# Three kinds of reordering in the opening of a fused attention and mixture-of-experts kernel: more weight slices converted early, one batch's loads issued later, and eight matmuls of block means moved

## The chip, the cores and the metric

The kernel runs on one core of one Trainium2 chip. The metric is the device time of the whole program in microseconds (us). Shorter is better.

A core has these engines, each with its own instruction queue, worked off in the order in which the program wrote it: PE (TensorE, matmuls; its weight loads are shown apart as PEld), DVE (VectorE), ACT (ScalarE), POOL (GpSimd) and SP (SyncE, which here only issues DMA transfers).

## The reference

Three stages follow each other. The sizes: 2 batches, 8 heads, 768 positions, head width 64, so 1536 tokens of width 512.

```python
def _attn_ref(q, k, v):
    block, window = (32, 16)
    k_sum = k.reshape(B, H, nb, block, D).max(axis=3)
    v_sum = v.reshape(B, H, nb, block, D).mean(axis=3)
    ...
    scores_all = np.concatenate([scores_l_m, scores_s], axis=-1)
    a = np.exp(scores_all)
    a = a / (np.sum(a, axis=-1, keepdims=True) + 1e-09)
    v_all = np.concatenate([v, v_sum], axis=2)
    return np.matmul(a, v_all).astype(np.float32)

def _moe_ref(x, w_in, w_out):
    h = x @ w_in
    relu6 = np.clip(h + 3.0, 0.0, 6.0)
    g = h * relu6 / 6.0
    return (g @ w_out).astype(np.float32)

def _moe2_ref(x, w_gate, w1, w2):
    logits = x @ w_gate
    ...
    for e in range(E):
        mask = assigned == e
        h = np.maximum(x[mask] @ w1[e], 0.0)
        out[mask] = h @ w2[e]
```

`w_in` is 512 x 2048. Each of the 8 experts takes 192 tokens, those of the highest logits first. Each query sees the keys nearer than 16 positions and, for each block of 32 keys, the block's maximum as a key and the block's mean as a value. `w_in`, `w_out` and `w_gate` arrive as 64-bit floats and are turned into 32-bit ones on the chip.

## The kernel before

**Tiles and units.** The tokens are 12 tiles of 128 (six to a batch). Three tiles make a unit, so there are four units. Unit `u` of the first dense stage (`gemm1(u)`) is 16 slices of `w_in`, and each slice is 12 matmuls of 128x384 on PE (lines 621 to 623), an ACT instruction (line 624) and a DVE instruction (the gate, line 637). The results of two neighbouring slices use two PSUM banks in turn, so slice `f + 2` can begin only when the gate of slice `f` is done. Attention runs one unit ahead: while `gemm1(u)` runs, the attention of unit `u + 1` is threaded between its slices. Attention of unit 0 has nothing to hide behind; it is written out by hand in `prologue()`.

**Attention of one tile** is two halves of four heads. For each half: `front` (8 score matmuls, line 383, then four DVE instructions, line 391, that add the mask and take the minimum), `soften` (exponentials on ACT, line 402; sums and reciprocals on DVE, lines 404 and 405; a POOL multiplication, line 406), `turn` (four transposes, line 414, and an ACT copy) and `values` (8 matmuls, line 429, from the V window `VW`). `window(n)` makes the key window of tile `n` with two DVE copies (line 368). `q_prep` transposes a tile of q (line 353) through PSUM bank 7 or 4; `values` of the even or odd tiles use the same banks. The block means of the first batch are 8 matmuls with a constant matrix (`vsum_mul`, line 199), after which `vsum_place` copies the result into both `VW` buffers (DVE, line 203, then ACT, line 204). No `values` product can run before that.

**The slices of `w_in`.** A slice is loaded as 512 KB (`w_in_load`, line 247) into one of four raw buffers. `w_conv` makes 32-bit floats of it with three DVE instructions (`f32_ops`, run at line 272); when the third is done, the load of the slice four later is queued. `w_split` cuts the result into a high part (ACT, line 289) and a low part (POOL, line 290), two slices after the conversion in the program's order (`CLAG`). `AHEAD` slices are converted while the prologue runs, the rest during unit 0.

**What sets the order.** `drive` interleaves several generators. Each has a total and a start and an end on a common scale; after each step the generator that is least far along goes next, and the numbers that the steps yield are how far each one went. They set only the order of the program text. Here `S0` and 1.0 are the start and the end of the conversions on the scale of the prologue. SP's queue is in the same order: a load that must wait for its buffer holds every load behind it.

**The second batch.** Its k and v come through the same buffers as the first batch's q and v (`load_rows("kraw", k, 1, j)`, 4 x 256 KB in pieces of 256 bytes, line 169, and `vsum_load(1, g)`, 2 x 768 KB, line 173). They are needed at the start of unit 1.

Of the kernel before, what the change touches and what calls it, by code (L numbers as in the profile page):

```python
# [16 lines left out]
HP = H // 2  # L17
# [9 lines left out]
UT = 3  # L27
# [16 lines left out]
SEEK, COUNT = 4600, 1900  # L44
ROUTE = 100000
CLAG = 2
AHEAD = 4
EARLY = 13
LEFT = 4
VLAG = 0  # L50
VN = 3
ATTS = [31212, 20565, 23910, 18810]
END = [0.92, 0.92, 0.92]
S0 = 0.27
S1 = 0.7
LX = 4
TAIL = [0, 1], [2]
# [31 lines left out]
def build(ctx, tc, q, k, v, w_in, w_out, w_gate, w1, w2, out):  # L89
# [30 lines left out]
    def bank(i):  # L120
        return psum.tile([128, 512], FT, name=f"bank{i}")
# [35 lines left out]
    q0 = early.take([H, UT, D])  # L157
# [6 lines left out]
    def load_rows(kind, src, b, i):  # L164
        if src is k:
            x = k1[i % 4]
        else:
            x = att.tile([128, H, D], FT, name="raw", bufs=3)
        SP.dma_start(x, src[b, :, i * 128:(i + 1) * 128, :].rearrange("h s d -> s h d"))
        raw[kind, b, i] = x  # L170

    def load_first(x, src, b, hs, rs, r):
        SP.dma_start(x[:, hs, rs], src[b, hs].rearrange("h (p r) d -> p h r d", r=r)[:x.shape[0], :, rs])

    def load_v(n):

        b, i = divmod(n, 6)
        for g in range(2):
            lo = i * 128 + g * QG - W
            a, z = max(lo, 0), min(lo + WIN, S)  # L180
            SP.dma_start(VW[n % 2][a - lo:z - lo, g], v[b, :, a:z, :].rearrange("h s d -> s h d"))
# [6 lines left out]
    def vsum(b):  # L188
        m = KR // 2
        while m:  # L190
            POOL.tensor_tensor(vs[:, :, :m], vs[:, :, :m], vs[:, :, m:2 * m], op=OP.add)
            m //= 2
# [13 lines left out]
    for g in range(2):  # L206
        hs = slice(HP * g, HP * g + HP)
        for rs in RH:
            load_first(k0, k, 0, hs, rs, KR)
        load_first(q0, q, 0, hs, slice(0, UT), UT)  # L210

    for x in VW:
        POOL.memset(x, 0.0)
# [88 lines left out]
    def kprep_first(g):  # L302
        hps = slice(2 * g, 2 * g + 2)
        for i, rs in enumerate(RH):
            for hp in range(2 * g, 2 * g + 2):
                p = bank((2, 3, 5, 6)[2 * i + hp % 2])
                for j in range(4):
                    for z in range(2):
                        PE.matmul(p[64 * z:64 * z + 64, j * KP:(j + 1) * KP], k0[:, 2 * hp + z, 4 * i + j], ident[:KP, :KP],  # L309
                                  start=True, stop=True, skip_group_check=True)  # L310
                ACT.activation(kT[:, hp, rs], p[:, :4 * KP].rearrange("p (r s) -> p r s", r=4), AF.Copy)
                DVE.tensor_reduce((ks if i else kmax)[:, hp], p[:, :4 * KP].rearrange("p (r n s) -> p n r s", r=4, s=4),
                                  axis=AX.XY, op=OP.max)
                yield 450
        DVE.tensor_tensor(ks[:, hps], ks[:, hps], kmax[:, hps], op=OP.max)

    def qprep_first(g):
        for hp in range(2 * g, 2 * g + 2):
            p = bank(7 if hp % 2 else 4)
            for i in range(UT):  # L320
                for z in range(2):
                    PE.matmul(p[64 * z:64 * z + 64, i * 128:(i + 1) * 128], q0[:, 2 * hp + z, i], ident,
                              start=True, stop=True, skip_group_check=True)
            ACT.activation(qT0[:, hp].rearrange("p (s r) -> p r s", r=UT), p[:, :U].rearrange("p (r s) -> p r s", r=UT), AF.Copy)
        if g:
            for n in range(UT):
                fr[n] = qT0[:, :, n * 128:(n + 1) * 128]
# [82 lines left out]
    def turn(n, h):  # L410
        A = Abuf[(2 * n + h) % (LAG + 1)]
        p = bank(2)
        for c in range(4):
            PE.transpose(p[:KEYS, c * 128:(c + 1) * 128], A[:, c], ident)  # L414
        at = att.tile([128, 4, 128], FT, name="at", bufs=3)
        ACT.activation(at[:KEYS], p[:KEYS].rearrange("p (c s) -> p c s", c=4), AF.Copy)  # L416
        ats[n, h] = at
# [35 lines left out]
    def halves():  # L453
        for n in range(UT, NT):
            b, i = divmod(n, 6)
            if b and i == 0:
                vsum(b)
                yield from kprep(b)
                q_prep(n)
                window(n)  # L460
                yield 2400
            for h in range(2):
                t = pend.pop(0) if len(pend) >= LAG else None
                if t:
                    turn(*t)
                    turned.append(t)
                    yield 660
                after = h == 1 and i < 5
                first = (n, h) == (UT, 1)
                if not first:  # L470
                    front(n, h, after)
                    yield 1250 + 450 * after
                pend.append((n, h))
                while turned:
                    if turned[0] == (6 * b, 0):
                        vsum_mul(0, True)
                        vsum_place()
                    values(*turned.pop(0))
                    yield 1000
                emit_x()  # L480
                if first:
                    yield 1
                    front(n, h, after)
                    yield 1250 + 450 * after
                yield from soften()
                emit_x()
                if (n, h) == (UT, 0):
                    for g in range(2):
                        vsum_load(1, g)
                    for j in range(4):  # L490
                        load_rows("kraw", k, 1, j)
            if i == 5:
                while pend or turned:
                    if turned:
                        yield 700
                        values(*turned.pop(0))
                        yield 1000
                        emit_x()
                    if pend:
                        yield 800  # L500
                        t = pend.pop(0)
                        turn(*t)
                        turned.append(t)
                        yield 660

    turned = []
    attention = halves()

    def attend_unit(u):
# [264 lines left out]
    def prologue():  # L774
        soft = []

        def half(n, h, after=False):
            front(n, h, after)
            soft.append(soften())
            next(soft[-1])  # L780
            pend.append((n, h))

        def rest():
            for _ in soft.pop(0):
                pass

        def turned_one():
            t = pend.pop(0)
            turn(*t)
            turned.append(t)  # L790

        for c in kprep_first(0):
            yield c
        qprep_first(0)
        window(0, slice(0, 2))
        yield 600
        for c in kprep_first(1):
            yield c
        half(0, 0)
        yield 1250  # L800
        qprep_first(1)
        window(0, slice(2, 4))
        yield 600
        half(0, 1, True)
        rest()
        yield 1250
        def block_means(i):
            for j in range(i, i + 2):
                vsum_mul(j, j == KR - 1)

        def both(t):
            values(*t)
            emit_x()

        half(1, 0)
        rest()
        yield 1250
        block_means(0)
        yield 1700
        turned_one()  # L820
        yield 660
        block_means(2)
        yield 1700
        half(1, 1, True)
        rest()
        yield 1700
        turned_one()
        yield 660
        block_means(4)
        yield 1700  # L830
        half(2, 0)
        rest()
        yield 1250
        block_means(6)
        vsum_place()
        yield 1700
        turned_one()
        yield 660
        for i in range(2):
            both(turned.pop(0))  # L840
            yield 1000
        half(2, 1, True)
        rest()
        yield 1700
        turned_one()
        yield 660
        both(turned.pop(0))
        yield 1000
        rest()
        yield from attend_unit(0)  # L850

    w_in_load(0)
    for g in range(2):
        vsum_load(0, g)
    w_in_load(1)
    load_v(0)
    load_v(1)
    for j in range(2, NW):
        w_in_load(j)
    for n in range(2):  # L860
        load_rows("qraw", q, 0, UT + n)

    def splits():
        for s in range(NF + CLAG):
# [7 lines left out]
    splitting, second = splits(), gemm2()  # L872
    drive([[prologue(), ATTS[0], 0, 1], [part(splitting, 4 * AHEAD), 4 * AHEAD, S0, 1.0]], soon)
    tlast = late = None
    for u in range(NU):
        st = []
        if u + 1 < NU:
            st = [[attend_unit(u + 1), ATTS[u + 1], -0.02, END[u]]]
            if u == 0:
                st.append([splitting, 4 * (NF - AHEAD) + CLAG, 0.0, S1])  # L880
        else:
# [422 lines left out]
```

## Time and profile before

| | |
|---|---|
| median of 3 runs | 585.88 us (585.55 to 587.0) |
| the profiled execution: its own time | 584.98 us |
| its span in the trace, first to last instruction | 583.0 us |
| busy share of the span: PE, DVE, ACT, POOL | 94%, 61%, 50%, 28% |
| mean granted clock of TensorE | 0.981 of full speed |

The profiled execution's own time is 0.9 us under the median, and 2.0 us of it lie around the span. The prologue is the first 50.0 us of the span; the 16 slices of unit 0 follow.

### The profile page before, as it was taken

How to read it: one execution, taken by the hardware profiler on the slowest of the kernel's cores; microseconds unless marked ns; L12 is line 12 of the kernel's file. 1: busy time of each engine (PE TensorE's matmuls, PEld its weight loads, DVE VectorE, ACT ScalarE, POOL GpSimd, SP SyncE). 2: the span in 40 equal slices, each digit the busy share in tenths (PEclk: the TensorE clock that was granted, in tenths of full speed). 3: DMA queues.
4: the chain of work that ended last, by engine and by line, in shares of the span. 5: the costliest groups of instructions: out<-in, count | busy, mean ns of one | idle time of the engine just before them, and what ended most of it. 6: DMA issues, size and time to landing. Idle time of an engine off the chain costs nothing.

```text
span 583.0 us, 10815 instructions
## 1 busy us (share of the span) xinstructions
PE 548.8 (94%) x3867; PEld 458.5 (79%) x3867; DVE 356.2 (61%) x1022; ACT 291.7 (50%) x698; POOL 163.9 (28%) x197
## 2 busy tenths in 40 slices
PE   6768789989999999999999999999999999999993
PEld 6447678879889989986677777778789888988882
DVE  6577795644543288750045655553588888888880
ACT  4556464456544445561132232234576777677750
POOL 1124348111111032582244444456001100111011
PEclk9789899999999999999999999999999999999998
DMA  9978962302110145430042000004589888998811
GB/s 235 231 193 171 276 177 48 77 20 47 28 36 19 47 141 176 140 105 2 1 126 91 1 1 1 1 18 183 155 262 289 251 242 249 288 254 233 255 47 33
DMA packets 98270, 75.05 MB, mean 129 GB/s; under 512 B 38112, under 2 KB 84704, under 8 KB 98208
## 3 DMA queue, kind: packets, MB, share of 16 engines
q1 hardware_dynamic: 96224, 67.96, 43.2%
q0 software_dynamic: 1984, 6.32, 3.0%
q8 instruction: 33, 0.54, 0.4%
q14 instruction: 29, 0.24, 0.1%
HBM read 67.55 MB, written 6.71 MB: 127 GB/s over the span
## 4 chain that ended last, share of the span: by engine, by line
PE 53%; issue 27%; DVE 8%; DMA 5%; POOL 3%; ACT 2%; SPq 0%; POOLq 0%; DVEq 0%; ACTq 0%
PE bank L738 8%; PE bank L739 7%; PE bank L740 7%; PE bank L621 6%; PE bank L622 5%; PE bank L623 5%; POOL out_dram L1107 3%; DVE bank L272 2%; PE bank L649 2%; PE bank L383 2%; PE bank L199 2%; PE bank L429 2%; PE bank L414 1%; DMA big<-in_moe_w_out_dram 1%; PE bank L309 1%
## 5 line engine op out<-in xcount | busy, mean ns | idle before, releaser
L621 PE MATMUL bank<-x,wh 128*128 128x384 f32 x256 | 91.7, 358 | 4.2 <-DVE t L637 2.1
L299 DVE TENSOR_TENSOR wl<-t,wh 128x1024 fp32r<-128x1024 f32 x64 | 77.0, 1220 | 20.5 <-ACT wh L298 18.1
L623 PE MATMUL bank<-x,wl 128*128 128x384 f32 x256 | 86.7, 339 | 2.5 <-POOL wl L290 2.5
L622 PE MATMUL bank<-x,wh 128*128 128x384 f32 x256 | 86.4, 338 | 0.4 <-DVE x L78 0.3
L715 ACT ACTIVATE thx<-t 128x384 fp32r<-128x384 f32 (+2 forms) x80 | 36.2, 459 | 94.6 <-PE bank L739 94.0
L624 ACT ACTIVATE t<-bank,three 128x384 f32<-128x384 f32 x64 | 37.1, 580 | 89.1 <-PE bank L623 87.1
L738 PE MATMUL bank<-wh,thx 128*128 128x512 f32 x192 | 79.2, 412 | 0.0
L716 POOL TENSOR_TENSOR tlx<-t,thx 128x384 fp32r<-128x384 f32 (+1 forms) x56 | 56.0, 1002 | 77.4 <-ACT thx L715 70.7
L740 PE MATMUL bank<-wh,tlx 128*128 128x512 f32 x192 | 75.3, 392 | 0.1
L739 PE MATMUL bank<-wl,thx 128*128 128x512 f32 x192 | 75.0, 390 | 0.0
L1132 PE MATMUL bank<-x,wh 128*128 128x384 f32 x256 | 73.7, 360 | 0.5 <-DVE x L1058 0.5
L298 ACT ACTIVATE wh<-t 128x1024 fp32r<-128x1024 f32 x64 | 65.6, 1047 | 0.0
L1134 PE MATMUL bank<-x,wl 128*128 128x192 f32 x256 | 64.2, 251 | 0.0
L637 DVE SCALAR_TENSOR_TENSOR t<-t,bank 128x384 f32<-128x384 f32 x64 | 34.9, 549 | 41.1 <-ACT t L624 41.1
L406 POOL TENSOR_TENSOR A<-A,sm 128x480 f32<-128x480 f32 x24 | 23.7, 987 | 128.0 <-ACT at L416 65.8
L1107 POOL DMA_INDIRECT out_dram<-t,idx x16 | 14.9, 931 | 141.5 <-DVE t L1156 136.0
L621 PEld LDWEIGHTS bank<-x,wh 128*128 128x128 f32 x256 | 48.2, 188 | 8.3 <-DVE t L637 3.1
L623 PEld LDWEIGHTS bank<-x,wl 128*128 128x128 f32 x256 | 48.3, 189 | 3.2 <-POOL wl L290 3.2
L622 PEld LDWEIGHTS bank<-x,wh 128*128 128x128 f32 x256 | 48.5, 189 | 1.0 <-DVE x L78 0.9
L1134 PEld LDWEIGHTS bank<-x,wl 128*128 128x128 f32 x256 | 48.9, 191 | 0.3
L1132 PEld LDWEIGHTS bank<-x,wh 128*128 128x128 f32 x256 | 48.1, 188 | 1.2 <-DVE x L1058 0.8
L1148 PE MATMUL bank<-wh,t 128*128 128x512 f32 x128 | 48.9, 391 | 0.0
(194 smaller groups left out, 1014.5 us busy)
## 6 DMA issues: line engine op xcount, KB each, us to landing
t<-in_moe_w_dram SPq DMA_DIRECT2D x128, 256.0 KB, 4.5
t<-in_moe_w_in_dram SPq DMA_DIRECT2D x16, 512.0 KB, 5.7
big<-in_moe_w_out_dram SPq DMA_DIRECT2D x16, 512.0 KB, 3.3
VW<-in_v_dram SPq DMA_DIRECT2D x20, 192.0 KB, 3.7
t<-in_v_dram SPq DMA_DIRECT2D x4, 768.0 KB, 11.8
raw<-in_q_dram SPq DMA_DIRECT2D x9, 256.0 KB, 4.7
t<-xs SPq DMA_DIRECT2D x8, 258.0 KB, 4.4
t<-in_k_dram SPq DMA_DIRECT2D x4, 384.0 KB, 6.0
```

The lines of the kernel that those rows point to most:

```text
L298: ACT.activation(hi, x, AF.Copy)
L299: DVE.tensor_tensor(lo, x, hi.bitcast(FT), op=OP.subtract)
L621: PE.matmul(p, wh[:, kk, :], xh[:, kk, :], start=kk == 0, stop=False)
L622: PE.matmul(p, wh[:, kk, :], xl[:, kk, :], start=False, stop=False)
L623: PE.matmul(p, wl[:, kk, :], xh[:, kk, :], start=False, stop=kk == KD - 1)
L716: (DVE if placed[0] else POOL).tensor_tensor(ths[i][1], t, ths[i][0].bitcast(FT), op=OP.subtract)
L738: PE.matmul(acc[j], th[:, c], WH[s], start=f == 0, stop=False)
L739: PE.matmul(acc[j], th[:, c], WL[s], start=False, stop=False)
L740: PE.matmul(acc[j], tl[:, c], WH[s], start=False, stop=f == NF - 1)
L1132: PE.matmul(p, a[:, kk, :], xt[:, kk].rearrange("p c s -> p (c s)"), start=kk == 0, stop=False, skip_group_check=True)
L1134: PE.matmul(p[:, :CAP], b[:, kk, :], xt[:, kk, 0, :], start=False, stop=kk == KD - 1, skip_group_check=True)
L1148: PE.matmul(p, x, w, start=m == 0 and i == 0, stop=m == NM - 1 and i == 2)
```

## The change

Nothing is computed differently; instructions change places.

- `AHEAD` goes from 4 to 7 and `S0` from 0.27 to 0.21.
- The second batch's v and k loads are issued after the second half of tile 4 instead of the first half of tile 3, k first.
- Both groups of the first q loads stand ahead of the second group of k loads, and the first of the later q tiles is loaded ahead of slices 2 and 3 of `w_in`.
- In the prologue both q preparations come before the second group of k transposes, the first half of tile 0 stands in the middle of that group, and the eight matmuls of block means stand after the fronts of tile 1 (2), after the first half of tile 2 (2) and after its second half (4).

```diff
-AHEAD = 4
+AHEAD = 7
-S0 = 0.27
+S0 = 0.21
...
-        load_first(q0, q, 0, hs, slice(0, UT), UT)
+        for i in range(2 if g == 0 else 0):
+            load_first(q0, q, 0, slice(HP * i, HP * i + HP), slice(0, UT), UT)
...
-                if (n, h) == (UT, 0):
+                if (n, h) == (4, 1):
+                    for j in range(4):
+                        load_rows("kraw", k, 1, j)
                     for g in range(2):
                         vsum_load(1, g)
-                    for j in range(4):
-                        load_rows("kraw", k, 1, j)
...
-        qprep_first(0)
+        for g in range(2):
+            qprep_first(g)
         window(0, slice(0, 2))
-        yield 600
-        for c in kprep_first(1):
+        yield 1200
+        for i, c in enumerate(kprep_first(1)):
             yield c
-        half(0, 0)
-        yield 1250
-        qprep_first(1)
+            if i == 1:
+                half(0, 0)
+                yield 1250
         window(0, slice(2, 4))
-        yield 600
         half(0, 1, True)
         rest()
-        yield 1250
+        yield 1850
...
         half(1, 0)
         rest()
         yield 1250
+        turned_one()
+        yield 660
+        half(1, 1, True)
+        rest()
+        yield 1700
         block_means(0)
         yield 1700
         turned_one()
         yield 660
+        half(2, 0)
+        rest()
+        yield 1250
         block_means(2)
-        yield 1700
-        half(1, 1, True)
-        rest()
         yield 1700
         turned_one()
         yield 660
+        half(2, 1, True)
+        rest()
+        yield 1700
         block_means(4)
         yield 1700
-        half(2, 0)
-        rest()
-        yield 1250
         block_means(6)
         vsum_place()
...
-    load_v(0)
-    load_v(1)
+    for n in range(2):
+        load_v(n)
+    load_rows("qraw", q, 0, UT)
     for j in range(2, NW):
         w_in_load(j)
-    for n in range(2):
-        load_rows("qraw", q, 0, UT + n)
+    load_rows("qraw", q, 0, UT + 1)
```

The lines of the changed kernel carry numbers one higher than before (272 becomes 273).

**SP's queue around the second batch's loads.** Before, from the V window of tile 3 on (`VW` is a V window, `raw` a tile of q, `t<-in_moe_w_in_dram` a slice of `w_in`, `t<-in_v_dram` and `t<-in_k_dram` the second batch):

```order
L181 DMA VW_95<-in_v_dram 96x8x64 x2
L173 DMA t<-in_v_dram 96x8x256 x2
L169 DMA t<-in_k_dram 128x8x64 x4
L247 DMA t<-in_moe_w_in_dram 128x4x256
L181 DMA VW_94<-in_v_dram 96x8x64 x2
L169 DMA raw<-in_q_dram 128x8x64
L247 DMA t<-in_moe_w_in_dram 128x4x256 x4
L169 DMA raw<-in_q_dram 128x8x64
L247 DMA t<-in_moe_w_in_dram 128x4x256
L181 DMA VW_95<-in_v_dram 96x8x64
L181 DMA VW_95<-in_v_dram 80x8x64
L247 DMA t<-in_moe_w_in_dram 128x4x256 x3
```

Now, from the loads of slices 11 to 13 on:

```order
L248 DMA t<-in_moe_w_in_dram 128x4x256 x3
L169 DMA raw<-in_q_dram 128x8x64
L248 DMA t<-in_moe_w_in_dram 128x4x256
L181 DMA VW_95<-in_v_dram 96x8x64
L181 DMA VW_95<-in_v_dram 80x8x64
L169 DMA t<-in_k_dram 128x8x64 x4
L173 DMA t<-in_v_dram 96x8x256 x2
L248 DMA t<-in_moe_w_in_dram 128x4x256
L181 DMA VW_94<-in_v_dram 80x8x64
```

Before, nine slices' loads stood behind the second batch's; now one does, that of slice 15, and the V window of tile 5 stands ahead.

**DVE around the copy into the V windows.** Before (`t<-t,bank` is the third instruction of a conversion, `VW_94` the copy at line 203):

```order
L272 SCALAR_TENSOR_TENSOR t<-t,bank_377 128x512
L203 COPY VW_94<-bank_339 24x1024
L272 TENSOR_SCALAR bank_425<-t 128x512
L272 SCALAR_TENSOR_TENSOR bank_425<-t,bank_425 128x512
L391 ISA A_92,sm<-bank_448,mask 128x120
```

Now:

```order
L406 RECIPROCAL sm<-sm 128x4
L273 SCALAR_TENSOR_TENSOR bank_428<-t,bank_428 128x512
L273 SCALAR_TENSOR_TENSOR t<-t,bank_428 128x512
L273 TENSOR_SCALAR bank_469<-t 128x512
L203 COPY VW_94<-bank_376 24x1024
L273 SCALAR_TENSOR_TENSOR bank_469<-t,bank_469 128x512
L273 SCALAR_TENSOR_TENSOR t<-t,bank_469 128x512
```

Ahead of the copy into `VW_94` there were 6 conversion instructions and there are now 13.

**PE around the last block means.** Before (L199 block means, L414 turn, L429 values, L383 front, L353 transposes of q):

```order
L199 MATMUL bank_339<-t,zones 120x512 x2
L414 MATMUL bank_417<-ident,A_92 120x128 x4
L429 MATMUL bank_427<-at,VW_94 64x64 x16
L383 MATMUL bank_448<-kw,t 64x120
L383 MATMUL bank_449<-kw,t 64x120
...
L353 MATMUL bank_458<-ident,raw 128x128 x4
L414 MATMUL bank_485<-ident,A_90 120x128 x4
L429 MATMUL bank_496<-at,VW_95 64x64 x8
```

Now:

```order
L354 MATMUL bank_440<-ident,raw 128x128 x4
L199 MATMUL bank_376<-t,zones 120x512 x4
L430 MATMUL bank_481<-at,VW_94 64x64 x16
L415 MATMUL bank_511<-ident,A_90 120x128 x4
L430 MATMUL bank_519<-at,VW_95 64x64 x8
L415 MATMUL bank_529<-ident,A_91 120x128 x4
```

The transposes of q now come ahead of the values product that takes the same bank, and four block means stand between the last front of tile 2 and that product.

## Rows read from the trace of the kernel before

**Rows 1.** PE's waits after 99 us: line, releaser, us, times, longest.

```profile
PE bank L429 <- issue: 1.4, 1, 1.4
```

**Rows 2.** PE in unit 0: start, us, line; in brackets idle before.

```profile
50.01 0.42 PE L621 MATMUL bank<-x,wh 128*128 128x384 f32 x1
...
66.33 0.41 PE L621 MATMUL bank<-x,wh 128*128 128x384 f32 x1 [0.99 <-DVE sm L404]
...
68.91 0.44 PE L623 MATMUL bank<-x,wl 128*128 128x384 f32 x1 [1.99 <-POOL wl L290]
...
80.13 0.41 PE L621 MATMUL bank<-x,wh 128*128 128x384 f32 x1 [1.00 <-ACT A L402]
...
83.34 0.44 PE L621 MATMUL bank<-x,wh 128*128 128x384 f32 x1 [0.31 <-DVE t L637]
...
87.43 0.44 PE L623 MATMUL bank<-x,wl 128*128 128x384 f32 x1 [0.56 <-POOL wl L290]
...
93.52 0.44 PE L621 MATMUL bank<-x,wh 128*128 128x384 f32 x1 [0.92 <-DVE t L637]
```

**Rows 3.** Stretches: busy us by engine, then clock, DMA share, GB/s.

```profile
20.00:36.00 16.00, 14.68 (x122) 7.75 (x117) 10.72 (x42) 7.68 (x29) 3.94 (x4) 0.83 0.95 229
36.00:50.00 14.00, 8.75 (x116) 7.11 (x117) 7.55 (x31) 7.78 (x25) 4.73 (x5) 0.76 0.61 141
...
70.00:73.00 3.00, 3.00 (x18) 2.56 (x21) 2.86 (x5) 1.15 (x3) 0.36 (x1) 0.50 1.11 312
```

**Rows 4.** DVE in order of time, prologue and unit 0.

```profile
28.71 0.96 DVE L368 COPY kw<-kT 128x384 f32<-128x384 f32 x2
...
32.99 1.23 DVE L203 COPY VW<-bank 24x1024 f32<-24x1024 f32 x1
...
64.31 0.69 DVE L272 TENSOR_SCALAR bank<-t 128x512 int32<-128x512 int32 x1 [3.21 <-DMA t<-in_moe_w_in_dram]
...
67.78 1.43 DVE L368 COPY kw<-kT 128x384 f32<-128x384 f32 x1
...
69.20 1.47 DVE L368 COPY kw<-kT 128x320 f32<-128x320 f32 x1
```

**Rows 5.** POOL in order of time, unit 0.

```profile
67.59 2.77 POOL L290 TENSOR_TENSOR wl<-t,wh 128x512 fp32r<-128x512 f32 x2
```

**Rows 6.** SP, the issue of DMAs in order of time.

```profile
35.35 0.91 SPq L181 DMA_DIRECT2D VW<-in_v_dram  x2
...
46.52 1.14 SPq L173 DMA_DIRECT2D t<-in_v_dram  x2
47.75 10.88 SPq L169 DMA_DIRECT2D t<-in_k_dram  x4
58.72 1.17 SPq L247 DMA_DIRECT2D t<-in_moe_w_in_dram  x1
```

**Rows 7.** DMA issues at 58.7 to 59.9 us: size, us from issue to landing.

```profile
t<-in_moe_w_in_dram SPq DMA_DIRECT2D x1, 512.0 KB, 5.5
```

**Rows 8.** DMA issues at 59.9 to 60.5 us.

```profile
VW<-in_v_dram SPq DMA_DIRECT2D x1, 192.0 KB, 5.1
```

**Rows 9.** DVE by line and shape, 20 to 99 us: busy us, mean ns, idle before.

```profile
L272 DVE SCALAR_TENSOR_TENSOR bank<-t,bank 128x512 int32<-128x512 int32 x16 | 11.1, 692 | 0.3
...
L637 DVE SCALAR_TENSOR_TENSOR t<-t,bank 128x384 f32<-128x384 f32 x13 | 7.1, 547 | 2.5 <-ACT t L624 2.5
...
L78 DVE TENSOR_TENSOR x<-bank,x 128x512 fp32r<-128x512 f32 x5 | 3.3, 665 | 0.9 <-ACT x L447 0.9
```

**Rows 10.** PE in order of time, prologue and tile 4.

```profile
34.27 1.15 PE L429 MATMUL bank<-at,VW 120*64 120x64 f32 x32 [1.32 <-DVE VW L203]
...
38.86 0.97 PE L353 MATMUL bank<-ident,raw 128*128 128x128 f32 x4 [2.86 <-issue]
...
44.61 1.69 PE L429 MATMUL bank<-at,VW 120*64 120x64 f32 x32
...
61.40 0.64 PE L383 MATMUL bank<-kw,qT 64*64 64x120 f32 x16
```

More of the change, by code (lines that the diff above doesn't have):

```diff
@@ L836, in prologue @@
         yield 1700
-        turned_one()
-        yield 660
+        rest()
         for i in range(2):
@@ L841, in prologue @@
             yield 1000
-        half(2, 1, True)
-        rest()
-        yield 1700
         turned_one()
@@ L848, in prologue @@
         yield 1000
-        rest()
         yield from attend_unit(0)
```

## The prediction

> **What bounds the kernel now.** I read the waits of PE first, then PE's own timeline. After 99 us PE waits for almost nothing: the longest group is 1.4 us, and the six groups that the view has for the remaining 484 us sum to 4.7 us [rows 1]. Whatever PE gains or loses before 99 us therefore goes through to the end nearly whole. So the question is when PE gets through the prologue and unit 0.
>
> Unit 0 begins at 50.01 us. Inside it PE stands idle six times [rows 2], in two clusters. The first, 0.99 and 1.99 us just before 66.33 and 68.91, goes back to DVE, which sat 3.21 us until 64.31 because the raw data of slice 7 had not landed [rows 4]. The clock followed: in 70 to 73 us TensorE was granted 0.50, its 1.2 GHz level, with all 3 us busy [rows 3], so 3 us of work of which half would have been saved at 2.4 GHz: 1.5 us. The second cluster, 1.00, 0.31, 0.56 and 0.92 us up to 93.52, is DVE and POOL running behind the slices. The sum of both is 2.98 + 1.5 + 2.79 = 7.3 us.
>
> Why slice 7 was late stands in SP's queue: the second batch's v loads are issued from 46.52 and its k loads from 47.75 for 10.88 us, and only then, at 58.72, the load of slice 7 [rows 6], which took 5.5 us to land [rows 7]. From the first v issue to that landing are 64.2 - 46.5 = 17.7 us.
>
> **The change part by part, up to the start of unit 0.** Three more slices are converted here. A conversion is three DVE instructions of about 0.69 us [rows 9] (the view has three such groups of 16), 2.06 us, so 6.2 us are added. DVE has 16 - 10.7 and 14 - 7.6, together 11.7 us, idle between 20 and 50 us [rows 3]; this is the cover. It covers the sum, not every place: ahead of the copy into the V windows there now stand 13 conversion instructions and not 6, so this copy (at 32.99 before, [rows 4]) can come up to 7 x 0.69 = 4.8 us later, and with it the values products of tile 0 (34.27, [rows 10]). Against that, PE's wait of 2.86 us ahead of the q transposes at 38.86 [rows 10] has no cause any more, since they now stand ahead of the product that takes the same PSUM bank. The eight block means are the same eight matmuls; only their place changes, at no price of their own as long as PE waits for DVE there. Bounds: 2.86 us gained, if DVE's idle time covers everything; 4.8 - 2.86 = 2.0 us lost, if it covers nothing. I take 0, near the middle, and unit 0 still begins at about 50.0. The reordered first q loads and the early q tile I cost at nothing: the k transposes that now come later are wanted later too, and if that cover failed it would be within those bounds.
>
> **In unit 0.** DVE has three conversions, 6.2 us, less to do after 50 us, and nothing stands ahead of slice 7's load any more. The first cluster goes, 4.5 us with its slow clock. The second cluster is 2.8 us of lag on an engine that is relieved of 6.2, so I let it go whole; if none of it went, that would be 2.8 us less. Slice 12, which began at 93.52, could then begin at 93.5 - 7.3 = 86.2.
>
> **What is late next.** Behind the moved loads SP has one more slice, 15. SP reaches the second batch when slice 14's load is issued, and this waits for conversion 10. In the new order conversion 10 follows the window copies of tile 4's second half, which before ended at 69.20 + 1.47 = 70.7 [rows 4]. Take off the 3.2 us of waiting and one conversion less ahead of it, 2.06: 65.4. From PE's side the front of that half starts at 61.40 [rows 10], and with its masking and the two slow copies (2.9 us) gives nearly the same. So conversion 10 ends at about 65.7 + 2.06 = 67.8, three further issues take SP to 69.1, and slice 15 lands 17.7 us after that as slice 7 did, at 86.8. DVE, stopped at this conversion, then has it (2.06), a low part (0.67) and the gate of slice 10 (0.55) [rows 9] to do: 90.1. Slice 12 needs the bank that this gate releases. PE waits 90.1 - 86.2 = 3.9 us, and the clock falls again as in 70 to 73 us, 1.5 us: 5.4 us are given back. Bounds of this term: 0, if the loads share the queues better than that, and 7.3, if everything that was gained is eaten.
>
> **Sum.** 0 - 7.3 + 5.4 = -1.9 us on the profiled execution's own 584.98, which makes 583.1. That execution lies 0.9 us under the median of the three runs, so 584.0 us on the median's scale.
>
> **A rule that speaks against it.** The two window copies at 67.78 and 69.20 took 1.43 and 1.47 us [rows 4] while POOL had low parts to make from 67.59 for 2.77 us [rows 5]; the pair at 28.71, with POOL idle, took 0.96 for both [rows 4]. The change puts POOL's work on slices 2 to 4 into the prologue, beside such copies. The Trainium skill, GPSIMD Engine Reference, "1. Specifications", says that GpSimd's SBUF interfaces are shared with VectorE and contended by DVE instructions in a two-port mode or with two SBUF inputs. The trace agrees with it in these rows. It gives a result of its own, which is the third rival.
>
> **The rivals.** First, slice 15 is not held. The 17.7 us included 10.88 us of issuing; if the DMA engines get through k and v in 12 us, the conversion finds its data and nothing is given back: 585.9 - 7.3 = 578.6. For it: w_in's pieces went at over 300 GB/s around 70 us [rows 3]. Against it: the same two loads held slice 7 by just this much.
>
> Second, the stall only moves. Slice 14's 512 KB and the V window of tile 5 are in the queues ahead of k, which they were not before; if they add 2 us, slice 15 lands at 89 and the gain is 0: 585.9. The same comes out if unit 0 begins 2 us late.
>
> Third, slower: DVE's chain in the prologue. With the three window copies of the prologue at the slow price (2.9 for 0.96 us, 1.9 each, 5.8 in all) and none of the 4.8 us covered, the values products of tile 0 come 10.6 us later. The V window of tile 2 is loaded behind them (35.35 before, [rows 6]); at 5.1 us to landing [rows 8] it would land at about 46 + 5 = 51, where its product before ran at 44.61 [rows 10]. Unit 0 would begin 6.4 us late, and after the 1.9 us of the sum 4.5 us are left: 590. It decides from a landing at 46.5, that is from about 6 us of delay of the products; 2 us past this gives 588.
>
> **How the numbers follow.** Within 0.3% (1.76 us), about what a measurement of this kernel can tell from no change, counts as the same. My forecast, the stall moved to slice 15 and partly given back, has 0.38; its own range is 582 to 586, so 0.22 of it is faster and 0.16 the same. The first rival has 0.20, all faster. The second has 0.22: 0.18 the same, 0.04 slower. The third has 0.20: 0.16 slower, 0.03 the same, 0.01 faster. Together faster 0.43, same 0.37, slower 0.20. The range goes from 579.5, just short of the first rival's full gain, to 588.0, the third rival 2 us past its point.
>
> **What the new trace would show.** Right: unit 0's first matmul within 2 us of 50.0; no wait of DVE at slice 7; no cluster of PE waits before 80 us; the second batch's k issued near 69; a wait of DVE for `t<-in_moe_w_in_dram` of some 3 us at conversion 15, near 84 to 87, and PE idle at slice 12 with a stretch at clock 0.50 behind it; slice 12 at about 90 to 91. First rival: no such wait, slice 12 near 86. Third: the copy into the V windows after 40 us, PE idle ahead of the values product of tile 2, and unit 0 beginning after 53. The prediction would be wrong if the prologue's order on ACT, which I have not costed apart from the bounds, moved the start of unit 0 by more than these bounds, or if the end of the kernel did not follow unit 0 one to one.

## The result, and the profile of the changed kernel

The change made the kernel slower: 591.84 us (587.96 to 592.75, 7 runs) against 586.70 us (585.55 to 587.08, 7 runs), a ratio of 1.0078 with a 95% interval of 1.0052 to 1.0105. The profiled execution took 592.75 us (span 590.6, mean clock 0.969), which is 7.8 us over the profiled execution of before; it is also the slowest of its seven.

In the changed kernel's own numbering lines from 211 on are one higher: the unit's matmuls are 622 to 624, `values` is 430, the conversions 273, the gate 638.

The waits of PE up to 110 us, changed kernel (us in total, times, longest):

```profile
PE bank L622 <- DVE t L638: 7.6, 2, 7.0
...
PE bank L430 <- issue: 2.9, 1, 2.9
...
PE bank L430 <- DMA VW<-in_v_dram: 0.8, 1, 0.8
```

One wait of 7.0 us stands where before there were the two clusters of [rows 2]. PE in order of time shows where it is, and that everything ahead of it is late too:

```profile
42.15 1.98 PE L430 MATMUL bank<-at,VW 120*64 120x64 f32 x32 [2.91 <-issue]
...
50.41 0.57 PE L430 MATMUL bank<-at,VW 120*64 120x64 f32 x12 [0.83 <-DMA VW<-in_v_dram]
...
55.14 0.67 PE L622 MATMUL bank<-x,wh 128*128 128x384 f32 x1
...
59.31 0.42 PE L622 MATMUL bank<-x,wh 128*128 128x384 f32 x1
...
62.16 0.44 PE L622 MATMUL bank<-x,wh 128*128 128x384 f32 x1
...
75.62 0.45 PE L622 MATMUL bank<-x,wh 128*128 128x384 f32 x1 [0.56 <-DVE t L638]
...
99.65 0.69 PE L622 MATMUL bank<-x,wh 128*128 128x384 f32 x1 [7.01 <-DVE t L638]
...
103.77 0.42 PE L622 MATMUL bank<-x,wh 128*128 128x384 f32 x1
```

Unit 0 begins at 55.14 instead of 50.01 [rows 2]. Its first slice takes 4.2 us (55.14 to 59.31), the second 2.9. Slice 12 begins at 99.65 and takes 4.1. The stretches (busy us of PE, PEld, DVE, ACT, POOL, then clock, DMA share, GB/s) show the clock at which this happened; in the first two, DVE's busy time is 12.05 and 11.74 where it was 10.72 and 7.55 [rows 3]:

```profile
20.00:36.00 16.00, 13.67 (x105) 8.13 (x106) 12.05 (x54) 8.08 (x36) 3.95 (x4) 0.68 0.96 228
36.00:50.00 14.00, 10.43 (x100) 6.85 (x98) 11.74 (x36) 8.02 (x22) 6.99 (x6) 0.76 0.73 198
50.00:60.00 10.00, 8.84 (x72) 8.08 (x73) 5.30 (x18) 4.31 (x13) 2.26 (x2) 0.66 0.84 181
...
99.00:103.00 4.00, 3.35 (x10) 3.35 (x11) 1.15 (x3) 1.10 (x2) 4.00 (x5) 0.50 0.00 0
```

The wait's releaser is named as the gate, but DVE in order of time shows the cause two steps back, a conversion without its data:

```profile
32.95 0.69 DVE L273 TENSOR_SCALAR bank<-t 128x512 int32<-128x512 int32 x1 [2.34 <-DMA t<-in_moe_w_in_dram]
...
37.50 0.96 DVE L369 COPY kw<-kT 128x384 f32<-128x384 f32 x2
...
40.82 1.23 DVE L203 COPY VW<-bank 24x1024 f32<-24x1024 f32 x1
...
96.25 0.69 DVE L273 TENSOR_SCALAR bank<-t 128x512 int32<-128x512 int32 x1 [7.86 <-DMA t<-in_moe_w_in_dram]
```

The last is the first instruction of slice 15's conversion, and the gate that PE waits for stands behind it. SP's queue, and the landing of the last load in it (KB, us from issue to landing):

```profile
40.09 3.88 SPq L248 DMA_DIRECT2D t<-in_moe_w_in_dram  x2
44.02 2.12 SPq L181 DMA_DIRECT2D VW<-in_v_dram  x2
...
76.71 4.98 SPq L169 DMA_DIRECT2D t<-in_k_dram  x4
81.75 2.04 SPq L173 DMA_DIRECT2D t<-in_v_dram  x2
83.88 0.79 SPq L248 DMA_DIRECT2D t<-in_moe_w_in_dram  x1
```
```profile
t<-in_moe_w_in_dram SPq DMA_DIRECT2D x1, 512.0 KB, 12.3
```

Slice 15's 512 KB were issued behind the second batch's k and v and landed at 96.2, 19.5 us after the first k load was issued.

**Where the 7.8 us came from.** Unit 0 begins 5.1 us later; its first slice at half clock costs 1.3 (4.2 less 2.9); the first cluster with its clock is gone, -4.5; of the second, 0.56 of 2.79 is left, -2.2; the new wait is +7.0, the half clock behind it +1.5. The sum is +8.2, against 7.8 between the two executions.

### The profile page after: what moved, and what is told of

It is laid out like the page before. It is cut to its first block, busy times and chain, and to the rows that moved or that the text cites. A ratio compares the mean times of both kernels' runs of the same rounds, so it can differ in the third digit from the quotient of the medians.

```text
span 590.6 us, 10807 instructions
## 1 busy us (share of the span) xinstructions
PE 554.5 (94%) x3867; PEld 464.3 (79%) x3867; DVE 356.2 (60%) x1022; ACT 292.0 (49%) x698; POOL 164.4 (28%) x197
## 4 chain that ended last, share of the span: by engine, by line
PE 52%; issue 26%; DMA 6%; DVE 5%; SPq 4%; POOL 3%; ACT 1%; POOLq 0%; DVEq 0%; ACTq 0%
PE bank L739 8%; PE bank L740 7%; PE bank L741 7%; PE bank L622 7%; PE bank L623 6%; PE bank L624 6%; DMA t<-in_moe_w_in_dram 3%; POOL out_dram L1109 3%; SPq L181 2%; PE bank L430 2%; PE bank L650 2%; PE bank L384 1%; DMA big<-in_moe_w_out_dram 1%; PE bank L574 1%; SPq L173 1%
## 5 line engine op out<-in xcount | busy, mean ns | idle before, releaser
L622 PEld LDWEIGHTS bank<-x,wh 128*128 128x128 f32 x256 | 49.1, 192 | 12.6 <-DVE t L638 9.7
L623 PEld LDWEIGHTS bank<-x,wh 128*128 128x128 f32 x256 | 49.3, 193 | 0.6 <-DVE x L78 0.5
L1134 PEld LDWEIGHTS bank<-x,wh 128*128 128x128 f32 x256 | 48.1, 188 | 1.2 <-DVE x L1060 0.8
```

Of the source, the lines that this page charges most:

```text
L622: PE.matmul(p, wh[:, kk, :], xh[:, kk, :], start=kk == 0, stop=False)
L623: PE.matmul(p, wh[:, kk, :], xl[:, kk, :], start=False, stop=False)
L1134: PE.matmul(p, a[:, kk, :], xt[:, kk].rearrange("p c s -> p (c s)"), start=kk == 0, stop=False, skip_group_check=True)
```

## The experiments

Ratios are to the kernel before, run beside each set: 586.16 us (kv_after_w15, kv_late_alone, ahead4_rest_new, ahead7_old_prologue), 586.06 (kv41_alone, kv_late_ahead7, kv_late_new_prologue, old_head_new_tail), 587.19 (k_only_41, new_head_old_tail, front_after_k, q_loads_early) and 588.63 (new_head_old_counts, old_head_new_counts). The expectations in us are written for a kernel before at about 586, so the last two are read by their ratios.

### Where the second batch's loads stand

**kv_after_w15**: the whole change, the second batch's loads at the next half, behind slice 15's load.

```diff
-                if (n, h) == (4, 1):
+                if (n, h) == (5, 0):
```

> The changed kernel with the second batch's k and v loads moved on once more, behind the load of slice 15 (after the first half of tile 5). Theory A, that slice 15 is held by these loads: DVE's wait of 7.9 us at conversion 15 and PE's 7.0 us at slice 12 go, and the slow clock behind them with about 2 us; 592 - 9 = 583. Rival A', that the wait only goes on to the next user (the k transposes of the second batch at the end of unit 0, about 100 us): PE waits some 5 us there and the time stays above 588.

Measured: 581.79 us, ratio 0.9912 (0.9881 to 0.9944), 10.05 us under the change. SP and the landing:

```profile
76.26 0.38 SPq L248 DMA_DIRECT2D t<-in_moe_w_in_dram  x1
76.70 5.24 SPq L169 DMA_DIRECT2D t<-in_k_dram  x4
81.99 2.04 SPq L173 DMA_DIRECT2D t<-in_v_dram  x2
```
```profile
t<-in_moe_w_in_dram SPq DMA_DIRECT2D x1, 512.0 KB, 4.8
```

Ahead of k and v the same load lands in 4.8 us instead of 12.3. Slice 12 begins at 90.85 and PE waits nowhere for longer than 0.55 us in unit 0, as theory A had it. Between the two profiled executions lie 10.6 us (592.75 and 582.14): 8.5 are the wait and its clock, and 1.7 are the start of unit 0, which is 53.4 here although the program is the same up to there, so variation between executions.

**kv41_alone**: the kernel before with this one part of the change.

```diff
-                if (n, h) == (UT, 0):
-                    for g in range(2):
-                        vsum_load(1, g)
+                if (n, h) == (4, 1):
                     for j in range(4):
                         load_rows("kraw", k, 1, j)
+                    for g in range(2):
+                        vsum_load(1, g)
```

> The kernel before with only the late k and v loads of the change (after the second half of tile 4, k first). Theory A: with four slices converted early, several slices' loads stand behind them, the wait goes from slice 7 to the first of these and is some 6 to 7 us of PE where it was 3 us; about 589. Rival: at that place the loads of the slices ahead are out far enough and the wait is no longer than the old one, 586.

Measured: 591.08 us, 1.0084 (1.0067 to 1.0101): as slow as the whole change. PE and SP:

```profile
94.56 0.69 PE L621 MATMUL bank<-x,wh 128*128 128x384 f32 x1 [6.37 <-DVE t L637]
```
```profile
74.15 5.56 SPq L169 DMA_DIRECT2D t<-in_k_dram  x4
79.77 2.04 SPq L173 DMA_DIRECT2D t<-in_v_dram  x2
81.91 2.15 SPq L247 DMA_DIRECT2D t<-in_moe_w_in_dram  x2
```

With four slices ahead two loads of `w_in` stand behind k and v, and the wait is at slice 11.

**kv_late_alone**: the same edit of the kernel before with `(5, 0)` in place of `(4, 1)`.

> The kernel before with nothing changed but the second batch's loads, put behind the load of slice 15. The wait at slice 7 goes (3 us of PE, 1.5 us of slow clock) and nothing else stands behind these loads: unit 0 begins at 50.0 and the time is 586.3 - 4.5 = 582. Rival: DVE's lag takes it back (PE's second cluster grows) and the time stays within 1 us of before.

Measured: 583.52 us, 0.9960 (0.9940 to 0.9980). The first cluster is gone; the second stays (1.49, 1.03, 0.32, 0.55 and 0.92 us). Unit 0 begins at 51.5 and not at 50.0, with the program of PE that the kernel before has up to there, and the time is 1.5 us over the expected 582.

**k_only_41**: the change with k at (4, 1) and v at (5, 0).

```diff
                     for j in range(4):
                         load_rows("kraw", k, 1, j)
+                if (n, h) == (5, 0):
                     for g in range(2):
                         vsum_load(1, g)
```

> The change, with only the four k loads of the second batch at unit (4, 1) and its two v loads at (5, 0), behind slice 15's load; so 1.05 MB stand ahead of slice 15's load instead of 2.6 MB. The change took 591.84 us and the wait at slice 12 7.0 us; with k and v both behind, 581.79 and 0. Theory (the hold of slice 15's load grows with the bytes ahead of it on the queue: 2.0 us of v's issues and most of v's 1.6 MB are gone): slice 15's load lands 6 to 8 us earlier, the wait at slice 12 falls to 0 to 2 us, time 582 to 586 us. Rival (it is k's small pieces that hold the queue, whatever the bytes): the wait stays at 5 to 7 us, time 589 to 592 us.

Measured: 583.07 us, 0.9924 (0.9901 to 0.9948). SP, then DVE at slice 15's conversion:

```profile
75.47 5.13 SPq L169 DMA_DIRECT2D t<-in_k_dram  x4
80.70 1.09 SPq L248 DMA_DIRECT2D t<-in_moe_w_in_dram  x1
81.84 1.44 SPq L173 DMA_DIRECT2D t<-in_v_dram  x2
```
```profile
87.07 0.69 DVE L273 TENSOR_SCALAR bank<-t 128x512 int32<-128x512 int32 x1
```

The conversion starts at 87.07 without a wait, so slice 15 had landed within 6.4 us of its issue at 80.70, with k's 1.05 MB still ahead of it. The rival, that k's pieces alone hold the queue, falls: without v's 1.6 MB ahead the hold is not seen.

### How many slices are converted ahead

**ahead4_rest_new** is the change with the edit below undone, **ahead7_old_prologue** the kernel before with it and the loads at (4, 1), **kv_late_ahead7** the same with the loads at (5, 0).

```diff
-AHEAD = 4
+AHEAD = 7
-S0 = 0.27
+S0 = 0.21
```

> The changed kernel with AHEAD = 4 and S0 = 0.27 again. Theory B, that the seven more conversion instructions ahead of the copy into the V windows make unit 0 begin 5.5 us late: it begins within 1.5 us of 50, and the time is about 588 (the wait at slice 15 stays). Rival B', that the new order of the q and k preparations and of the block means does it: it begins after 53 us and the time is 591 or more.

> The changed kernel with the prologue's order, the first loads' order and the early q tile as before, so AHEAD = 7, S0 = 0.21 and the late k and v loads alone. Theory B: unit 0 begins after 53 us, about 591. Rival B': it begins near 50 to 51 us, about 587.

> The kernel before with AHEAD = 7, S0 = 0.21 and the second batch's loads behind the load of slice 15; old prologue. If the three conversions' cost in the prologue (unit 0 begins 2.7 us later) is more than paid back in unit 0 by DVE's lag that goes: under the 583.5 of the late loads alone, about 580.5. Rival: DVE's lag was no bound, then 583.5 + 2.7 = 586.

Measured: 588.83 us, 1.0038 (1.0018 to 1.0058); 588.92 us, 1.0041 (1.0028 to 1.0054); 579.31 us, 0.9886 (0.9869 to 0.9904). With the loads at (4, 1) PE waits 7.1 us at slice 11 in the first and 6.5 at slice 12 in the second; the number of slices ahead only moves the place. Unit 0 begins at 50.5 in the first, as theory B had it, and at 52.7 in the second, between its two expectations, and the time there misses both (591 and 587). With the loads out of the way seven slices instead of four are worth 4.2 us (583.52 to 579.31), and the second cluster is down to one wait of 0.55.

### The prologue

**kv_late_new_prologue** is kv_after_w15 with `AHEAD` 4 and `S0` 0.27. **old_head_new_tail** is kv_after_w15 with the prologue's head, the steps up to the first `rest()`, and the first q loads as before:

```diff
-        for g in range(2):
-            qprep_first(g)
+        qprep_first(0)
         window(0, slice(0, 2))
-        yield 1200
-        for i, c in enumerate(kprep_first(1)):
+        yield 600
+        for c in kprep_first(1):
             yield c
-            if i == 1:
-                half(0, 0)
-                yield 1250
+        half(0, 0)
+        yield 1250
+        qprep_first(1)
         window(0, slice(2, 4))
+        yield 600
         half(0, 1, True)
         rest()
-        yield 1850
+        yield 1250
```

> The kernel before with the new prologue and first loads, four slices early, and the second batch's loads behind slice 15. Rival B' (the new order alone makes unit 0 late): unit 0 begins after 53 us and the time is above 586. Theory B: unit 0 begins within 1.5 us of the same kernel with the old prologue, and the time is within 1.5 us of its 583.5.

> The changed kernel with the second batch's loads behind slice 15 and the prologue's first part (q and k preparations, the first front of tile 0, the first q loads) as before; the block means' new places, the early q tile and AHEAD = 7 stay. If the 2.6 us by which the second front of tile 0 came late is from the preparations' order: unit 0 begins some 2 us earlier than with them (53.4) and the time is about 579.5. Rival: DVE's 13 conversion instructions set the values products of tile 0 whatever the first part does, 581.5 to 582.

Measured: 581.30 us, 0.9919 (0.9902 to 0.9935), unit 0 at 47.4; and 577.99 us, 0.9866 (0.9848 to 0.9884), unit 0 at 48.0. Neither expectation for the first holds: unit 0 begins 4.1 us ahead of kv_late_alone's, and the time is 2.2 us less. With four slices ahead the change's prologue is not late; with seven it is (unit 0 at 53.4, 581.79 us), and with the old head it is not.

Three runs take that head apart. **new_head_old_tail** is kv_after_w15 with the block means and later fronts where they were before. **front_after_k** is kv_after_w15 with `half(0, 0)` and its `yield 1250` behind the loop over `kprep_first(1)` instead of inside it. **q_loads_early** is old_head_new_tail with the change's first q loads:

```diff
-        load_first(q0, q, 0, hs, slice(0, UT), UT)
+        for i in range(2 if g == 0 else 0):
+            load_first(q0, q, 0, slice(HP * i, HP * i + HP), slice(0, UT), UT)
```

> k and v behind slice 15, seven slices ahead, the change's head (order of q's and k's preparations and loads), but the block means and the fronts of the later tiles where they were before. Old head with old tail gave 579.31 us, old head with new tail 577.99, new head with new tail 581.79. Theory (the head costs about 3.8 us by itself, the tail gives 1.3): 582 to 584.5 us, unit 0 at 52 to 55 us. Rival (the head costs only together with the new places of the block means): 578.5 to 580.5 us, unit 0 at 50 to 51.5 us.

> The version with the old head, the new tail and k and v behind slice 15 (577.99 us) with one step of the change's head: q's preparations and loads as in the change, but the first half of tile 0's front behind all of k's preparation instead of between its pieces. The change's own head in the same place gave 581.79 us, unit 0 at 53.4 us instead of 48.0. Theory (the exponentials of the early front stand ahead of k's last copies on ScalarE, and that makes front (0, 1) and all behind it late): without them 577.5 to 579.5 us, unit 0 at 48 to 50 us. Rival (the order of q's loads and preparations does it, or the pieces are late for another reason): 580.5 to 583 us, unit 0 at 51 us or later.

> The version with the old head, the new tail and k and v behind slice 15 (577.99 us), but q's first loads in the change's order (both ahead of k's second group). Theory (the loads' order is not what costs, since q's and k's first loads have landed before the preparations want them): 577 to 579 us, unit 0 at 47 to 49.5 us. Rival (the later load of k's second group makes the head late): 580 to 583 us, unit 0 at 51 us or later.

Measured: 583.25 us, 0.9929 (0.9902 to 0.9956), unit 0 at 53.5; 581.75 us, 0.9907 (0.9877 to 0.9936), unit 0 at 53.1; 578.25 us, 0.9841 (0.9819 to 0.9862), unit 0 at 50.0. The head costs with either tail. My theory that the exponentials of the early front do it falls, and so, by its time, does the order of q's loads (its unit 0 begins 0.5 us past the range of the theory). What was left: the order of the preparations, or the numbers that the head yields (1200, 1250, 0, 1850 instead of 600, 1250, 600, 1250), 600 more in sum, by which `drive` brings a conversion forward.

**new_head_old_counts** and **old_head_new_counts** are the two missing corners.

```diff
         window(0, slice(0, 2))
-        yield 600
+        yield 1200
...
         window(0, slice(2, 4))
-        yield 600
         half(0, 1, True)
         rest()
-        yield 1250
+        yield 1850
```

(as for the second; the first undoes the same in kv_after_w15)

> kv_after_w15 (the whole change with k and v behind slice 15's load, 581.79 us) with only the head's counts of time for the planner set back: 600, 1250, 600 and 1250 ns behind the steps as before, instead of 1200, 1250, 0 and 1850; the order of the preparations and of q's loads stays that of the change. By the counts a conversion, and the load that it makes room for, comes a place earlier on VectorE and on SP. Theory (the counts cost: SP issues two w_in loads, the second one only when its conversion is over, ahead of the V windows of tile 2): with one w_in load ahead, the V windows are issued at 40 to 41.5 us, unit 0 at 48 to 50.5 us, time 577 to 579.8 us. Rival (q's second preparation ahead of k's second half costs, since the first fronts are some 1 us later): unit 0 at 52 us or later, time 580.5 to 583 us.

> old_head_new_tail (577.99 us, unit 0 at 48.0 us) with only the head's counts of time for the planner as in the change: 1200, 1250, 0 and 1850 ns instead of 600, 1250, 600 and 1250; the preparations and q's loads stay as before. Theory (the counts cost): two w_in loads ahead of the V windows of tile 2 on SP, unit 0 at 51 to 53.5 us, time 580.3 to 583 us. Rival (the order of the preparations costs): unit 0 at 48 to 50 us, time 577 to 579.5 us.

Measured: 580.92 us, 0.9868 (0.9838 to 0.9897), unit 0 at 50.4; and 584.24 us, 0.9933 (0.9917 to 0.9950), unit 0 at 52.1. By ratios the new counts cost 0.44 points with the new head (0.9912 and 0.9868) and 0.67 with the old (0.9933 and 0.9866), 2.6 and 3.9 us. The second difference is clear of the intervals, the first is not, since they overlap. The order of the preparations costs nothing that shows (with old counts 0.9868 against 0.9866 and, with the same q loads, 0.9841, whose intervals overlap). In SP's order the counts do this (`-` old_head_new_tail, `+` old_head_new_counts), the same with either head:

```
 L169 DMA raw<-in_q_dram 128x8x64
+L247 DMA t<-in_moe_w_in_dram 128x4x256 x2
+L181 DMA VW_94<-in_v_dram 96x8x64 x2
+L247 DMA t<-in_moe_w_in_dram 128x4x256
+L181 DMA VW_95<-in_v_dram 96x8x64 x2
 L247 DMA t<-in_moe_w_in_dram 128x4x256
 L181 DMA VW_94<-in_v_dram 96x8x64 x2
-L247 DMA t<-in_moe_w_in_dram 128x4x256 x2
-L181 DMA VW_95<-in_v_dram 96x8x64 x2
-L181 DMA VW_94<-in_v_dram 96x8x64 x2
-L247 DMA t<-in_moe_w_in_dram 128x4x256
```

One more load of `w_in` stands ahead of the V windows of tile 2, and it cannot be issued before the conversion that frees its buffer is over. SP, then PE of old_head_new_tail:

```profile
36.81 0.37 SPq L247 DMA_DIRECT2D t<-in_moe_w_in_dram  x1
39.40 0.91 SPq L181 DMA_DIRECT2D VW<-in_v_dram  x2
```
```profile
38.14 1.44 PE L429 MATMUL bank<-at,VW 120*64 120x64 f32 x32 [2.42 <-issue]
...
44.31 0.57 PE L429 MATMUL bank<-at,VW 120*64 120x64 f32 x12 [0.20 <-DMA VW<-in_v_dram]
...
48.01 0.42 PE L621 MATMUL bank<-x,wh 128*128 128x384 f32 x1
```

And the same of old_head_new_counts:

```profile
37.18 3.88 SPq L247 DMA_DIRECT2D t<-in_moe_w_in_dram  x2
41.11 2.17 SPq L181 DMA_DIRECT2D VW<-in_v_dram  x2
```
```profile
39.24 1.15 PE L429 MATMUL bank<-at,VW 120*64 120x64 f32 x32 [1.63 <-issue]
...
46.46 0.34 PE L429 MATMUL bank<-at,VW 120*64 120x64 f32 x4 [2.55 <-DMA VW<-in_v_dram]
47.28 0.57 PE L429 MATMUL bank<-at,VW 120*64 120x64 f32 x12 [0.48 <-DMA VW<-in_v_dram]
...
52.14 0.67 PE L621 MATMUL bank<-x,wh 128*128 128x384 f32 x1
```

The first product comes 1.1 us later, the V windows are issued 1.7 later and seen by PE about 3 later, with 3.0 us of waiting instead of 0.2; then PE goes on at half clock, the first slice of the unit included. Of the 1.7 us at most 0.7 is SP held by the load (the product that frees the window ends at 40.4 and the issue is at 41.11); the 1.1 is the conversion instruction that now stands ahead of the copy, with what varies between executions.

The traces of all the kernels, one execution each, sort by this load. From the first matmul of tile 0's products to the first of unit 0 they took, in us (in the old tail the block means and the later fronts stand where they were before):

| | |
|---|---|
| old tail | before 15.7, kv41_alone 16.6, kv_late_alone 15.4, kv_late_ahead7 15.3, ahead7_old_prologue 15.3, new_head_old_tail 15.4 |
| new tail, one load of `w_in` between the last load of q and the V windows of tile 2 | kv_late_new_prologue 9.3, old_head_new_tail 9.9, q_loads_early 9.9, ahead4_rest_new 10.1, new_head_old_counts 10.4 |
| new tail, two such loads | kv_after_w15 12.4, front_after_k 12.7, old_head_new_counts 12.9, the change 13.0, k_only_41 13.6 |

So the start of the products, right behind the copy into the V windows, goes through to unit 0 nearly one to one; the new tail shortens the rest by 5 to 6 us, and the second load takes about 3 of these back. From the issue of tile 2's V windows to the product that waited for them it is 4.8 to 5.1 us with one load (q_loads_early does not wait) and 5.8 to 6.7 with two. New_head_old_counts, then new_head_old_tail:

```profile
39.98 1.98 PE L430 MATMUL bank<-at,VW 120*64 120x64 f32 x32 [2.40 <-issue]
...
46.90 0.57 PE L430 MATMUL bank<-at,VW 120*64 120x64 f32 x12 [1.14 <-DMA VW<-in_v_dram]
...
50.40 0.42 PE L622 MATMUL bank<-x,wh 128*128 128x384 f32 x1
```
```profile
38.09 1.97 PE L430 MATMUL bank<-at,VW 120*64 120x64 f32 x32 [2.77 <-DVE VW L203]
...
53.48 0.42 PE L622 MATMUL bank<-x,wh 128*128 128x384 f32 x1
```

## Why the prediction was wrong

**The prologue term failed.** "I take 0 ... Bounds: 2.86 us gained ... 2.0 us lost": it was 5.1 us lost between the two profiled executions, and 1.3 more by the clock of the first slice. Executions differ: where PE's program is the same up to there, unit 0 begins at 50.01, 50.75 and 51.53 (before, kv41_alone, kv_late_alone) and at 55.14, 53.43 and 54.48 (the change, kv_after_w15, k_only_41), on average 3.6 us later, which is past the bound too. Three sizes were wrong:

- The copy into the V windows slipped by 7.8 us, from 32.99 [rows 4] to 40.82, and by 6.7 in kv_after_w15 (39.67), where I had 4.8 at most. I had counted the seven conversion instructions alone. With the block means moved, the masking of one more half of a tile and one more pair of window copies (the pair at 37.50) stand ahead of the copy as well, and in this execution conversion 2 waited 2.34 us for its data.
- The new order gains more than the 2.86 us that I named: by the table above 5 to 6 us behind the start of tile 0's products. PE now stands 2.91 us ahead of these products instead, at 42.15.
- What a conversion issues I left out, at a price of nothing. Its end queues a `w_in` load on SP, and one such load more ahead of the V windows of tile 2 takes about 3 us back.

In the changed kernel the products begin 7.9 us later and the rest is 2.7 us shorter (15.7 to 13.0): the 5.1. The prologue's order on ACT, which I named as the place where I could be wrong, costs nothing that shows (front_after_k, 0.9907 against 0.9912). The counts, which I did not price at all, cost 3.9 us with the old head; with the new one their 2.6 are not clear of the intervals.

**The steps in unit 0 held.** No wait of DVE at slice 7, no PE waits before 75 us, one of 0.56 at 75.62: both clusters went, as predicted. Without the new wait slice 12 would have begun at 92.6 (99.65 less 7.01); that is the predicted 86.2 and the 6.4 us (5.1 and 1.3) by which the unit was late.

**The step "what is late next" had the mechanism and not the size.** Slice 15 was held, the wait stood at slice 12 by way of conversion 15 and the gate, and the slow clock behind it cost 1.5 us, as predicted. But the wait was 7.0 us where I had 3.9. The 3.1 us divide in two: k's first load came at 76.71, and not at 69.1 and 6.4 later, 75.5: 1.2; and the landing took 19.5 us from there, not 17.7: 1.8. The upper bound, "7.3, if everything that was gained is eaten", was none: what the hold costs depends on the queue, not on what was gained elsewhere, and it was 8.5 with the clock.

**The rivals.** The first, no hold, falls by kv_after_w15 against the change. The second had the right kind of failure, a late unit 0, and too small a price. The third had the right path, from a late copy by late products to the V window of tile 2, for the wrong reason: the window copies ahead of it were not slow (the pair at 37.50 took 0.96 us). It also read the 44.61 of [rows 10] as the product of tile 2, while this group opens with the second half of tile 1. By whole versions, the change without its counts and with the loads at (5, 0) is worth -1.32 points (new_head_old_counts, 0.9868), the counts give back 0.44 (to 0.9912) and the loads' place 1.66 (to 1.0078): -7.7, +2.6 and +9.7 us, together the 4.6 us by which the ratio is over 1 on 586.7.

**What stays open.** With the old tail (new_head_old_tail) the V windows are issued early, at 39.89, and unit 0 begins at 53.5 all the same: its products begin 3.8 us later than before, at 38.09, and the way from there is the old one, 15.4 us. Which part of the new order makes that way 5 to 6 us shorter I have not separated, nor how the 3 us of the second load divide between SP, the landing and the slow clock. What the block means' new places are worth in the whole time, 1.3 us (579.31 to 577.99), is inside the intervals.

**What beats both.** Three versions with k and v at (5, 0) and seven slices ahead lie within each other's reach: old_head_new_tail 0.9866, q_loads_early 0.9841, new_head_old_counts 0.9868. The last is the whole change with two corrections, the loads one half tile later and the old counts.

## What to carry to other kernels

When a step moves, list what its end releases, above all the loads that it queues, and look at which load in the same queue is wanted first; a bulk load that nobody needs for 20 us belongs behind the last one that somebody does. A number that only sets the order of a program is part of the change and has to be priced like one. And a long wait of PE has two prices, itself (7.0 us here) and the slow clock behind it (1.5).

## What the runs showed of the hardware that I had not expected

One and the same 512 KB load took 4.8 us with k and v behind it and 12.3 with them ahead, while in the changed kernel the queues moved 199 to 235 GB/s in each stretch of 4 us from 76 to 96; with k's 1.05 MB alone ahead of it no wait is seen.

Copies of DVE and POOL's low parts do disturb each other, in these rows only where they meet in time. In the changed kernel POOL, and DVE above, just miss each other:

```profile
36.09 1.27 POOL L291 TENSOR_TENSOR wl<-t,wh 128x512 fp32r<-128x512 f32 x1 [0.20 <-ACT wh L290]
38.89 0.99 POOL L407 TENSOR_TENSOR A<-A,sm 128x480 f32<-128x480 f32 x1 [1.53 <-DVE sm L406]
```

In q_loads_early they meet, POOL first and then DVE, and the same pair takes 1.75 us instead of 0.96:

```profile
34.30 1.27 POOL L291 TENSOR_TENSOR wl<-t,wh 128x512 fp32r<-128x512 f32 x1 [1.57 <-ACT wh L290]
```
```profile
34.62 1.75 DVE L369 COPY kw<-kT 128x384 f32<-128x384 f32 x2
```

This pair agrees with the sharing of GpSimd's SBUF interfaces with VectorE that the Trainium skill states (GPSIMD Engine Reference, "1. Specifications"). It did not decide the case.
